# Mask product one phase after its exponentials, row turns in later steps, a fourth PSUM bank from the fusion on, and batch 1's dilated turns by DMA

## The chip, the cores and the metric

The kernel runs on one core of one Trainium2 chip. The metric is the device time of one execution in microseconds (us). The kernel before took 256.71 us, the median of 7 runs (256.2 to 257.37).

## The reference

Windowed attention over 8 batches, 8 heads, 576 positions and 64 dimensions a head, followed by a multiplicative feed-forward network over the 4608 tokens. Heads 0 to 3 see the last 32 positions ("plain"), heads 4 to 7 every fourth of the last 128 ("dilated").

```python
scores = scale * np.matmul(q, k.transpose(0, 1, 3, 2))
mask_plain = (rel >= 0) & (rel < window)
mask_dil = (rel >= 0) & (rel < window * dilation) & (rel % dilation == 0)
scores = np.where(masks[None, :, :, :], scores, -1000000000.0)
attn = np.exp(scores - np.max(scores, axis=-1, keepdims=True))
attn = attn / (np.sum(attn, axis=-1, keepdims=True) + 1e-09)
x = np.matmul(attn, v)      # to (4608, 512), heads side by side
a = x @ w1                  # 512 -> 1024
b = x @ w2
out = (a * b @ w3) @ w_out  # 1024 -> 1024 -> 512
```

## The kernel before, in words

The instructions are placed by hand: each engine executes what it is given in the order in which the program issues it. TensorE's stream is the feed-forward network of one batch; the attention of a later batch is cut into small phases that are put between its matmuls.

*The network.* `ffn1(b, hf, f)` makes one 128 x 288 block of a * b: four matmuls with w1 into a PSUM bank, a cast to `asb` on ScalarE (L612), four with w2 into another bank, and on VectorE the gate product of the bank and `asb` into `gt` (L619). Its matmuls (L579) read `XT[1]` (dilated heads, chunks 2 and 3) first and `XT[0]` (plain heads) after. `ffn2` multiplies 128 tokens by the fused weights (L646), ScalarE copies the bank to `osb` (L653, six buffers) and SP's queue stores it. The fused weights w3 w_out are made once, by `fuse_t` (turns of w3 on TensorE, copied by ScalarE) and `fuse_m` (L676, copied to `wf_sb` by VectorE at L684). Batch 0's ffn1 runs until about 37 us with banks of its own. Then come the fusion (to 55.7 us), batch 0's first four ffn2 tiles (to about 64 us), and from there ffn1 of batches 1 to 7 with the ffn2 tiles that come due, some 27 us a batch.

*Banks.* `bank()` gives out the banks of a pool of three in turn. From the moment `late["x"]` is set, every fourth call gives `ps_x`, a bank set aside. Before the change this is set after batch 1. Until then `ps_x` serves `fuse_t(0)` and the turns in `to_channels`, and for the turns it goes on doing so.

*The attention.* A `Step` is one batch, one kind of heads (u = 1 dilated, 0 plain) and one half of the positions; a batch has the four steps d0, d1, p0, p1. `transposes` turns rows of q and k (loaded by POOL's queue) so that the head dimension lies on partitions, by VectorE (L277, L269): four pieces each for q and dilated k, two for plain k. `scores` issues 24 small matmuls into `ps_a`, their exponentials into `et` on ScalarE (L343), and the product with the 0/1 mask in place on VectorE (L344). `values` multiplies `et` by v (L355), and VectorE takes reciprocals (L363) and scales into `xo` (L366, five buffers). `to_channels` turns `xo` into `XT`: by six turns on TensorE (L413) into `ps_x` and a copy by ScalarE (L419), or, where `by_dma` is set, by one transposing DMA on SP's queue (L404). Before the change that is for batches above 2 and the dilated steps of batch 2.

*Phases.* `later(f)` makes a phase and `behind(f)` adds to the last one. `second_batch` lists the phases of batch 1 with the point at which each is issued; `segment` makes those of batches 2 to 7. In `segment` each phase has a width (`after`), and `point(n)`, called before each product of ffn1 (0.57) and each half of an ffn2 tile or of a `fuse_m` (1), counts points and issues all phases that are due. A batch is 27.25 points. `marks` fixes by which point each batch's last step must be done; `ahead` moves that point earlier. Phase by phase, a step in `segment` is: its scores; an empty phase with two row turns behind it; the turns of the step two back; the values of the step before; an empty phase with two more row turns. `prefetch` issues the loads of a batch that is two ahead.

Of the kernel before, what the change touches and what calls it, by code (L numbers as in the profile page):

```python
# [12 lines left out]
BF16 = mybir.dt.bfloat16  # L13
# [3 lines left out]
ACT = mybir.ActivationFunctionType  # L17
# [6 lines left out]
HALF = 288  # L24
# [29 lines left out]
def kernel(  # L54
# [11 lines left out]
    nc = tc.nc  # L66
# [6 lines left out]
    KFF = d_ff // P  # L73
    NT = n_tok // TB
    scale = 1.0 / float(np.sqrt(D))
# [42 lines left out]
    ps_x = psum.tile([P, 2 * TB], BF16, name="ps_x")  # L118
    pool = four_banks()
    ps_s = [pool.tile([P, 2, TB], F32, name=f"ps_s{i}") for i in range(2)]  # L120
    late = {}

    def bank():
        if "x" in late:
            late["x"] += 1
            if late["x"] % 4 == 0:
                return ps_x.bitcast(F32)
        return banks.tile([P, TB], F32, tag="f", name="f")
# [163 lines left out]
    class Step:  # L292
        def __init__(self, n, b, u, hf):
            self.b, self.u, self.hf = b, u, hf
            self.et = ets[n % NET]

            self.by_dma = b > 2 or (b == 2 and u == 1)
            self.xo = {}

        def score_matmuls(self, heads, bank_of, start):  # L300
# [36 lines left out]
        def scores(self):  # L337

            ps_a = late["a"]
            self.score_matmuls(range(4), lambda h: ps_a[:, h], True)  # L340
            ev = self.probs(0, 4)
            mk = (mask_di if self.u else mask_pl[:, self.hf]).rearrange("p m x -> p (m x)")
            nc.scalar.activation(out=ev, in_=ps_a[:, :, 0:HALF], func=ACT.Exp, scale=scale)  # L343
            nc.vector.tensor_tensor(  # L344
                out=ev, in0=ev, in1=mk.unsqueeze(1).to_broadcast([P, 4, HALF]), op=AL.mult
            )
# [51 lines left out]
                        self.value_matmul(2 * hp + hl, m, ov[:, j // 3, j % 3, :])  # L398
            self.normalize(ov, self.xo.rearrange("p h j d -> p (h j) d"), 4, 3)()

        def to_channels(self, ps=ps_x, copy=nc.scalar.copy, hps=(0, 1)):
            dst = XT[self.u][:, 2 * self.b + self.hf]
            if self.by_dma:
                nc.sync.dma_start(  # L404
                    out=dst.rearrange("p h (m t) -> p (h m) t", m=3),
                    in_=self.xo[0:96].rearrange("p h (m e) d -> p (h m) (e d)", m=3),
                    transpose=True,
                )
                return
            xv = ps[:, 0 : 2 * HALF].rearrange("p (h x) -> p h x", h=2)  # L410
            for hp in hps:
                for m in range(3):
                    nc.tensor.transpose(  # L413
                        out=xv[:, hp, 96 * m : 96 * m + 96],
                        in_=self.xo[0:96, hp, 2 * m : 2 * m + 2, :],
                        identity=ident[0:96, 0:96],
                    )
            h = slice(hps[0], hps[-1] + 1)
            copy(out=dst[:, h], in_=xv[:, h])  # L419
# [3 lines left out]
    steps = [  # L423
        Step(4 * b + 2 * (1 - u) + hf, b, u, hf)
        for b in range(B)
        for u in (1, 0)
        for hf in range(2)
    ]
# [10 lines left out]
    def later(f, *args, after=1.0):  # L439

        phases.append([lambda: f(*args)])
        room.append(after)
# [5 lines left out]
    def first_batch():  # L448


        d0, d1, p0, p1 = steps[0:4]
        transpose_qk(0, 1, 0)
        transpose_qk(0, 1, 1)
        d0.scores_of_pair(0)
        d0.scores_of_pair(1)
        transpose_qk(0, 0, 0)
        d1.scores_of_pair(0)
        d1.scores_of_pair(1)
        transpose_qk(0, 0, 1)
        warm_up(4)  # L460
        p0.scores_of_pair(0)
        p0.scores_of_pair(1)
        warm_up(2)
        d0.values_of_pair(0)
        d0.values_of_pair(1)
        p1.scores_of_pair(0)
        warm_up(1)
        d1.values_of_pair(0)
        d1.values_of_pair(1)
        p1.scores_of_pair(1)  # L470
        d0.to_channels()
        p0.values_of_pair(0)
        p1.values_of_pair(0)
        pool = four_banks()
        ps_b = [pool.tile([P, TB], F32, name=f"ps_b{i}") for i in range(4)]
        late.update(b=ps_b, n=0)
        d1.to_channels(ps_b[0].bitcast(BF16))
        warm_up(1, ps_b[3])
        p0.values_of_pair(1)
        p0.to_channels(ps_x, hps=(0,))  # L480
        p1.values_of_pair(1)
        begin(0, 0, (2, 3))
        begin(0, 1, (2, 3))
        begin(0, 0, (0,))
        begin(0, 1, (0,))
        p0.to_channels(ps_x, hps=(1,))
        x1 = bank().bitcast(BF16)
        p1.to_channels(x1, nc.vector.tensor_copy, hps=(0,))
        begin(1, 0, (2, 3))
        begin(1, 1, (2, 3))  # L490
        begin(0, 0, (1,))
        begin(0, 1, (1,))
        p1.to_channels(x1, nc.vector.tensor_copy, hps=(1,))
        begin(1, 0, (0,))
        begin(1, 1, (0,))
        ffn1(0, 0, 0)
        begin(1, 0, (1,))
        begin(1, 1, (1,))
        const_masks()
        prefetch(2)  # L500
# [3 lines left out]
    def second_batch():  # L504

        d0, d1, p0, p1 = steps[4:8]
        for at, f, *args in (
            (19, transpose_qk, 1, 1, 0),
            (20, transpose_qk, 1, 1, 1),
            (22, d0.scores),  # L510
            (24, d1.scores),
            (26, d0.values),
            (26, transpose_qk, 1, 0, 0),
            (27, transpose_qk, 1, 0, 1),
            (28, d0.to_channels),
            (28, d1.values),
            (31, p0.scores),
            (32, d1.to_channels),
            (33, p1.scores),
            (35, p0.values),  # L520
            (37, p0.to_channels),
            (37, p1.values),
            (37, prefetch, 3),
            (37, transpose_qk, 2, 1, 0),
            (38, transpose_qk, 2, 1, 1),
            (39, p1.to_channels),
            (39, transpose_qk, 2, 0, 0),
        ):
            later(f, *args)
            when.append(at)  # L530

    def segment(lo, hi):


        pieces = []

        def some():
            for f in pieces[:2]:
                behind(f)
            del pieces[:2]  # L540

        for i in range(lo, hi + 1):
            at, b = i % 4, i // 4
            more = 4 * (b + 1) < hi
            if at == 0 and i < hi:
                pieces += transposes(b, 0, 1)
                for u, which in ((1, 0), (1, 1), (0, 0)) if more else ():
                    pieces += transposes(b + 1, u, which)
            if i < hi:
                later(steps[i].scores, after=0.8)  # L550
                later(lambda: None, after=0.8)
                some()
            if i > lo + 1 and not steps[i - 2].by_dma:
                later(steps[i - 2].to_channels, after=0.4)
                done_at[i - 2] = len(phases)
            if i > lo:
                later(steps[i - 1].values, after=0.8)
                if steps[i - 1].by_dma:
                    behind(steps[i - 1].to_channels)
                done_at[i - 1] = len(phases)  # L560
                if i < hi:
                    later(lambda: None, after=0.8)
                    some()
            if at == 2:
                behind(prefetch, b + 2)

# [89 lines left out]
    w3T = {}  # L656

    def fuse_t(ft):
        xv = bank().bitcast(BF16) if ft else ps_x
        xv = xv.rearrange("p (g x) -> p g x", g=KFF)  # L660
        for g in range(KFF):
            nc.tensor.transpose(  # L662
                out=xv[:, g, :],
                in_=w3n[ft // 2][:, ft % 2, g * P : (g + 1) * P],
                identity=ident,
            )
        w3T[ft] = wk_pool.tile([P, KFF, P], BF16, tag="w3T", bufs=3, name="w3T")
        nc.scalar.copy(out=w3T[ft], in_=xv)
# [44 lines left out]
    n0 = len(when)  # L713
    marks = [(40, n0)]
    for b in range(2, B):
        ahead = (0, 3, 6)[min(b - 2, 2)]
        marks.append((40 + 27.25 * (b - 1) - ahead, done_at[4 * b + 3]))
    place = np.concatenate([[0.0], np.cumsum(room)])
    xs, ys = [m[0] for m in marks], [place[m[1]] for m in marks]
# [1 line left out]
    def point(n):  # L721
        state[0] += n
        want = int(np.searchsorted(place, np.interp(state[0], xs, ys) - 1e-6))
        while state[1] < want and (state[1] >= n0 or state[0] >= when[state[1]]):
            for f in phases[state[1]]:
                f()
            state[1] += 1

    for f in range(1, KFF + 2):
        if f < KFF:  # L730
            ffn1(0, 0, f)
        if f == KFF:
            fuse_t(0)
        if f >= 2:
            ffn1(0, 1, f - 2)
# [14 lines left out]
    for b in range(1, B):  # L750
        for hf in range(2):
            for f in range(KFF):
                ffn1(b, hf, f, point)
                if due and f in (1, 3, 5):
                    ffn2(due.pop(0), point)
            while P * (done + 1) <= b * S + (hf + 1) * HALF:
                due.append(done)
                done += 1
        if b == 1:
            late["x"] = 0  # L760
    for t in due:
        ffn2(t, point)
    assert state[1] == len(phases)
# [30 lines left out]
```

## Time and profile before

| | us |
|---|---|
| median of 7 runs | 256.71 (256.2 to 257.37) |
| the profiled execution | 256.57 |
| its span | 254.8 |
| TensorE, scores of one step (24 matmuls) | 0.44 |
| exponentials of one step, L343 | 1.13 |
| mask product, L344 | 0.76 |
| gate product, L619 | 0.50 |
| cast of a bank, L612 | 0.40 |
| reciprocals and scaling, L363 and L366 | 0.22 and 0.95 |
| row turn, L277 (q and dilated k) | 0.42 |
| copy of six turns, L419 | 0.64 |

Busy time of the engines by stage, and what the DMA engines moved (the share is the sum of packet times over 16 engines, so that it can go above one):

| stage, us | TensorE | VectorE | ScalarE | POOL | DMA share | GB/s |
|---|---|---|---|---|---|---|
| 40.0 to 55.7 | 15.41 | 11.96 | 9.73 | 8.75 | 1.42 | 198 |
| 55.7 to 68.3 | 12.34 | 9.38 | 7.52 | 6.19 | 1.50 | 217 |
| 68.3 to 95 | 26.42 | 20.04 | 13.38 | 6.13 | 1.73 | 187 |
| 95 to 122 | 27.00 | 18.10 | 12.99 | 5.48 | 0.98 | 146 |
| 122 to 149 | 27.00 | 19.30 | 12.82 | 5.48 | 0.94 | 135 |
| 149 to 176 | 27.00 | 18.57 | 12.96 | 4.07 | 0.69 | 100 |

A matmul's record runs from its start to its end, and the next one starts before that end; so an engine that waits a little between two matmuls can still be counted as busy. The distance between starts tells more than the busy share. In the waits, a line reads: engine and line that waited, what it waited for, us in total, number of times, longest.

### The profile page before, as it was taken

Reading aid. Unit: us, or ns where it says so; the run is one execution under the profiler, and the core shown is the slowest. Engines: PE = TensorE matmul, PEld = TensorE weight load, DVE = VectorE, ACT = ScalarE, POOL = GpSimd, SP = SyncE. Lnnn points to the kernel's source line nnn. Section 1 sums busy time; section 2 is a strip of 40 time slices with the busy share of each in tenths; the row PEclk is TensorE's granted clock in tenths of the full one; section 3 lists DMA queues with packets and bytes.
Section 4 is the critical chain, followed back from the end, with each engine's and each line's share of the span. In section 5 each row is a group of like instructions: output and inputs, shape, how many; then the busy total and the mean of one; then the engine's idle time right before and its main releaser. Section 6 shows DMA issues by size and latency. Waiting matters only on the chain.

```text
span 254.8 us, 6683 instructions
## 1 busy us (share of the span) xinstructions
PE 249.2 (98%) x2700; PEld 165.4 (65%) x2700; DVE 160.9 (63%) x379; ACT 119.3 (47%) x220; POOL 59.9 (23%) x87
## 2 busy tenths in 40 slices
PE   7999999999999999999999999999999999999995
PEld 2467774645676766667676766676767666777663
DVE  6676436867878766657685866576767543645550
ACT  2464456564644554554545454454444445333332
POOL 8884333747206200511061106000000000000000
PEclk9999999999999999999999999999999999999999
DMA  6999999999999993999479968922314122312113
GB/s 103 166 186 199 207 213 198 190 203 199 256 192 141 174 221 106 134 185 155 111 101 164 177 106 124 169 67 44 88 26 104 48 64 67 106 32 76 41 44 123
DMA packets 66562, 33.81 MB, mean 133 GB/s; under 512 B 51556, under 2 KB 56932, under 8 KB 66532
## 3 DMA queue, kind: packets, MB, share of 16 engines
q0 software_dynamic: 47232, 20.70, 69.0%
q1 hardware_dynamic: 19300, 12.69, 20.0%
q8 instruction: 21, 0.34, 0.6%
q14 instruction: 9, 0.07, 0.1%
HBM read 41.39 MB, written 9.44 MB: 199 GB/s over the span
## 4 chain that ended last, share of the span: by engine, by line
PE 78%; DMA 12%; DVE 3%; ACT 2%; POOL 2%; issue 1%; POOLq 0%
PE f L579 32%; PE f L646 19%; PE ps_x L579 9%; DMA qn<-in_q_dram 6%; PE ps_x L646 5%; PE ps_a L355 4%; PE f L676 4%; PE ps_a L313 4%; DMA w_sb<-in_moe_w_dram 3%; DMA kn<-in_k_dram 2%; ACT et L343 2%; POOL w_sb L177 1%; PE f L662 1%; PE ps_x L413 1%; DVE gt L619 1%
## 5 line engine op out<-in xcount | busy, mean ns | idle before, releaser
L579 PEld LDWEIGHTS <-w_sb 128*128 128x128 bf16 x1024 | 97.2, 98 | 30.9 <-issue 2.0
L579 PE MATMUL f<-XT,w_sb 128*128 128x288 bf16 x704 | 100.5, 286 | 0.5 <-DVE gt L619 0.2
L619 DVE TENSOR_TENSOR gt<-f,asb 128x288 bf16<-128x288 f32 x91 | 45.1, 503 | 17.9 <-PE f L579 17.8
L646 PE MATMUL f<-wf_sb,gt 128*128 128x512 bf16 (+1 forms) x240 | 55.9, 372 | 0.0
L612 ACT CAST asb<-f 128x288 bf16<-128x288 f32 x85 | 33.9, 399 | 33.4 <-PE f L579 31.1
L646 PEld LDWEIGHTS <-gt 128*128 128x128 bf16 x296 | 27.7, 98 | 25.5
L343 ACT ACTIVATE et<-ps_a 128x1152 bf16<-128x1152 f32 x28 | 31.7, 1131 | 10.4 <-PE ps_a L313 10.4
L653 ACT COPY osb<-f 128x512 f32<-128x512 f32 (+1 forms) x30 | 17.1, 571 | 39.8 <-PE f L646 37.7
L166 POOL DMA_DIRECT2D vd<-in_v_dram x32 | 21.3, 673 | 53.0 <-PE ps_a L355 46.2
L579 PE MATMUL ps_x<-XT,w_sb 128*128 128x288 bf16 x192 | 31.4, 286 | 0.0
L366 DVE TENSOR_TENSOR xo<-ps_a,rcp 96x768 bf16<-96x768 f32 x28 | 26.7, 954 | 1.0
L344 DVE TENSOR_TENSOR et<-et,mask_pl 128x1152 bf16<-128x1152 bf16 x14 | 10.6, 758 | 19.2 <-ACT et L343 19.2
L277 DVE STREAM_TRANSPOSE qt<-qn 128x160 uint32<-128x160 uint32 (+1 forms) x64 | 21.2, 422 | 2.3 <-DMA qn<-in_q_dram 2.2
L344 DVE TENSOR_TENSOR et<-et,mask_di 128x1152 bf16<-128x1152 bf16 x14 | 10.6, 758 | 17.8 <-ACT et L343 17.8
L355 PEld LDWEIGHTS <-et 128*128 128x128 bf16 x384 | 16.0, 98 | 3.4 <-ACT et L333 0.2
L313 PEld LDWEIGHTS <-kt 32*128 32x128 bf16 x768 | 10.6, 93 | 11.4 <-issue 8.6
L579 PE MATMUL ps_b<-XT,w_sb 128*128 128x288 bf16 x128 | 16.5, 286 | 0.0
L612 ACT CAST asb<-ps_x 128x288 bf16<-128x288 f32 x27 | 10.8, 398 | 11.2 <-PE ps_x L579 11.2
L676 PE MATMUL f<-wo_sb,w3T 128*128 128x512 bf16 x64 | 16.0, 380 | 0.0
L646 PE MATMUL ps_x<-wf_sb,gt 128*128 128x512 bf16 x56 | 13.2, 379 | 0.0
L619 DVE TENSOR_TENSOR gt<-ps_x,asb 128x288 bf16<-128x288 f32 x21 | 10.1, 483 | 4.3 <-PE ps_x L579 4.3
L313 PE MATMUL ps_a<-qt,kt 32*128 32x96 bf16 x672 | 12.4, 202 | 0.3 <-DVE kt L277 0.3
(71 smaller groups left out, 179.2 us busy)
## 6 DMA issues: line engine op xcount, KB each, us to landing
out_dram<-osb SPq DMA_DIRECT2D x28, 144.0 KB
qn<-in_q_dram POOLq DMA_DIRECT2D x6, 576.0 KB, 9.9
kn<-in_k_dram POOLq DMA_DIRECT2D x6, 576.0 KB, 10.3
w_sb<-in_moe_w_dram POOLq DMA_DIRECT2D x8, 256.0 KB, 7.9
w3n<-in_moe_w_dram POOLq DMA_DIRECT2D x4, 512.0 KB, 14.0
vp<-in_v_dram POOLq DMA_DIRECT2D x5, 384.0 KB, 7.4
out_dram<-osb SPq DMA_DIRECT2D x10, 128.0 KB
qn<-in_q_dram POOLq DMA_DIRECT2D x4, 288.0 KB, 6.6
```

What stands on the lines that cost most here:

```text
L166: nc.gpsimd.dma_start(out=vds[b % 2][p0 : p0 + n, 4 * m : 4 * m + 4, 16 : 16 + 2 * D], in_=bass.AP(tensor=x.tensor, offset=x.offset + (4 * ...
L277: nc.vector.transpose(out=bass.AP(tensor=o.tensor, offset=o.offset + at, ap=[o.ap[0], [1, n], [9, 16], [step, 2]],), in_=t[:, k : k + 4 * ...
L313: nc.tensor.matmul(out=bank_of(h)[:, c0 : c0 + 96], lhsT=kt[prt, 96 * m : 96 * m + P, c], rhs=rhs, start=(start and c == 0), stop=(c == 1 ...
L343: nc.scalar.activation(out=ev, in_=ps_a[:, :, 0:HALF], func=ACT.Exp, scale=scale)
L344: nc.vector.tensor_tensor(out=ev, in0=ev, in1=mk.unsqueeze(1).to_broadcast([P, 4, HALF]), op=AL.mult)
L355: nc.tensor.matmul(out=out, lhsT=self.et[:, c0 : c0 + P], rhs=rhs, start=True, stop=True)
L366: nc.vector.tensor_tensor(out=xo[0:96].rearrange("p (n k) d -> p n k d", n=n), in0=ov[0:96, :, :, x0 : x0 + D], in1=rcp[0:96].unsqueeze(3) ...
L579: nc.tensor.matmul(out=ps[:, 0:HALF], lhsT=w_sb[:, c, f * P : (f + 1) * P], rhs=x, start=(c == 2), stop=(c == 1),)
L612: nc.scalar.copy(out=a_sb, in_=ps[:, 0:HALF])
L619: nc.vector.tensor_tensor(out=g, in0=pb, in1=a_sb, op=AL.mult)
L646: nc.tensor.matmul(out=y, lhsT=gt[:, f, g0 : g0 + P], rhs=wf_sb[:, f, c0 : c0 + n], start=(f == 0), stop=(f == KFF - 1),)
L676: nc.tensor.matmul(out=wf_ps[ft], lhsT=w3T[ft][:, g, :], rhs=wo_sb[:, g, :], start=(g == 0), stop=(g == KFF - 1),)
```

## The change

Five edits.

1. The mask product leaves `scores` and becomes a phase of its own, `mask`, where the empty phase after the scores was (in batch 1 it gets points of its own, one after those of the scores).
2. The row turns of a batch's four steps, before two behind each of the two empty phases, are issued in the numbers (2, 0), (0, 2), (3, 3), (2, 2): the first number behind the scores, the second at the end of the step.
3. `late["x"]` is set before the loop of batch 0's ffn1, so that the fusion, batch 0's first ffn2 tiles and batch 1's ffn1 have four banks in turn. `fuse_t(0)` and the turns of `to_channels` take their bank from the rotation.
4. The dilated steps of batch 1 are turned by DMA.
5. `ahead` of batch 3 is 4 points where it was 3.

```diff
-            self.by_dma = b > 2 or (b == 2 and u == 1)
+            self.by_dma = b > 2 or (b > 0 and u == 1)
...
             ev = self.probs(0, 4)
+            nc.scalar.activation(out=ev, in_=ps_a[:, :, 0:HALF], func=ACT.Exp, scale=scale)
+
+        def mask(self):
+            ev = self.probs(0, 4)
             mk = (mask_di if self.u else mask_pl[:, self.hf]).rearrange("p m x -> p (m x)")
-            nc.scalar.activation(out=ev, in_=ps_a[:, :, 0:HALF], func=ACT.Exp, scale=scale)
             nc.vector.tensor_tensor(
...
-        def to_channels(self, ps=ps_x, copy=nc.scalar.copy, hps=(0, 1)):
+        def to_channels(self, ps=None, copy=nc.scalar.copy, hps=(0, 1)):
...
+            if ps is None:
+                ps = bank().bitcast(BF16)
...
             (22, d0.scores),
+            (23, d0.mask),
             (24, d1.scores),
+            (25, d1.mask),
...
             (32, d1.to_channels),
+            (32, p0.mask),
             (33, p1.scores),
+            (34, p1.mask),
...
-        def some():
-            for f in pieces[:2]:
+        def some(n):
+            for f in pieces[:n]:
                 behind(f)
-            del pieces[:2]
+            del pieces[:n]
...
+            n = ((2, 0), (0, 2), (3, 3), (2, 2))[at]
             if i < hi:
                 later(steps[i].scores, after=0.8)
-                later(lambda: None, after=0.8)
-                some()
+                some(n[0])
+                later(steps[i].mask, after=0.8)
...
                 if i < hi:
                     later(lambda: None, after=0.8)
-                    some()
+            if i < hi:
+                some(n[1])
...
-        xv = bank().bitcast(BF16) if ft else ps_x
-        xv = xv.rearrange("p (g x) -> p g x", g=KFF)
+        xv = bank().bitcast(BF16).rearrange("p (g x) -> p g x", g=KFF)
...
-        ahead = (0, 3, 6)[min(b - 2, 2)]
+        ahead = (0, 4, 6)[min(b - 2, 2)]
...
+    late["x"] = 0
     for f in range(1, KFF + 2):
...
-        if b == 1:
-            late["x"] = 0
```

Left out: `first_batch` now names `ps_x` in its one call of `to_channels` that had it by default, so nothing changes there.

More of the change, by code (lines that the diff above doesn't have):

```diff
@@ L470, in first_batch @@
         p1.scores_of_pair(1)
-        d0.to_channels()
+        d0.to_channels(ps_x)
         p0.values_of_pair(0)
```

## The prediction

> **What bounds the kernel now.** I read the page's shares first, then who waited for whom, then TensorE's own timeline, and the chain last, to see where the timeline's gaps stop.
>
> ```profile
> PE 249.2 (98%) x2700; PEld 165.4 (65%) x2700; DVE 160.9 (63%) x379; ACT 119.3 (47%) x220; POOL 59.9 (23%) x87
> ...
> PEclk9999999999999999999999999999999999999999
> ```
>
> TensorE is called busy for 98% of the span at the full clock, so only its own work or gaps hidden inside its busy time can give anything back.
>
> ```profile
> DVE et L344 <- ACT et L343: 37.0, 27, 2.8
> ```
>
> VectorE stood 37.0 us, in 27 waits, with a mask product at the head of its queue whose exponentials were not done: 1.37 us each. Everything behind it waits too, such as the gate products (L619) that free a PSUM bank. What that costs must be read on TensorE.
>
> ```profile
> 41.51 1.04 PE L676 MATMUL f<-wo_sb,w3T 128*128 128x512 bf16 x4
> 42.54 0.62 PE L662 MATMUL f<-ident,w3n 128*128 128x128 bf16 x8
> ...
> 49.06 0.42 PE L413 MATMUL ps_x<-ident,xo 96*128 96x96 bf16 x6
> 49.31 0.53 PE L355 MATMUL ps_a<-vd,et 128*128 128x65 bf16 x12
> ...
> 64.29 2.34 PE L579 MATMUL f<-XT,w_sb 128*128 128x288 bf16 x16
> 66.56 0.44 PE L313 MATMUL ps_a<-qt,kt 32*128 32x96 bf16 x24
> 66.94 1.15 PE L579 MATMUL f<-XT,w_sb 128*128 128x288 bf16 x8
> 68.30 1.79 PE L579 MATMUL f<-XT,w_sb 128*128 128x288 bf16 x12 [0.21 <-DVE gt L619]
> 69.92 0.53 PE L355 MATMUL ps_a<-vd,et 128*128 128x65 bf16 x12
> 70.29 2.28 PE L579 MATMUL f<-XT,w_sb 128*128 128x288 bf16 x16
> 72.51 0.44 PE L313 MATMUL ps_a<-qt,kt 32*128 32x96 bf16 x24
> 72.88 3.11 PE L579 MATMUL f<-XT,w_sb 128*128 128x288 bf16 x20
> ...
> 91.22 1.89 PE L646 MATMUL f<-wf_sb,gt 128*128 128x512 bf16 x8
> 93.18 0.41 PE L413 MATMUL ps_x<-ident,xo 96*128 96x96 bf16 x6
> ```
>
> Each line is a run of matmuls: start, length, count. Undisturbed, a 288-column matmul starts every 0.1225 us (four in 0.49) and the last one shows 0.286, so a run of n should last 0.1225 n + 0.16; a 512-column one starts every 0.216.
>
> ```profile
> 126.32 1.47 PE f L579 x12
> 127.79 0.49 PE ps_x L579 x4
> ```
>
> These are such undisturbed lines of the chain (12 x 0.1225 = 1.47, the next run follows at once). From 95 us to the end I find no start late by over 0.04 us. There bank() already hands out four banks, ps_x among them. Before 95 us the runs are too long.
>
> **The change, part by part.**
>
> *Fourth bank from the fusion on, and the mask a phase later.* The excess, run by run: 42.54 should have been 41.51 + 4 x 0.216 = 42.37, so 0.16; the run at 64.29, 2.34 against 2.12, 0.21; 68.30 against 66.94 + 0.98, 0.37; inside the run at 68.30, 1.79 against 1.63, 0.16; at 70.29, 0.16; at 72.88, 3.11 against 2.61, 0.49 in two stalls; two more runs at 83.90 and 87.69, 0.21 and 0.12 by the same sum; and 93.18 should have been 91.22 + 1.73, so 0.23. The sum is 2.11 us. The stalled matmuls waited for ScalarE's casts or for VectorE, that is, for a bank. With a fourth bank each asks for its bank one product (0.49 us) later, and no single stall is longer than 0.37. The mask product moves behind at least part of the work that it held up. I count 2.11 gained; bounds 1.0 (if the waits for VectorE, about half of it, come back elsewhere) and 2.11. After 95 us the later mask gains nothing, because TensorE shows no gap there to fill. A fifth stall, 0.35 at 41.13, waits for the row turns of batch 1, which wait for a load until 39.02; it stays.
>
> *Batch 1's dilated turns by DMA.* Two groups of six turns leave TensorE: 49.06 to 49.31, 0.25 each, 0.50 together, both behind the load-bound point at 41.13, so on the path. Two copies of 0.64 leave ScalarE, which gains nothing by itself. Added are two issues on SP's queue, which has nothing to do between 44 and 58.20 us, the first store. The stores queue behind the turns: their first rows land from 61.87 now, and up to 3 us later does not matter, since six osb buffers let the seventh tile, at about 93 us, be the first to wait. Batch 1's first product at 64.29, earlier by 0.16 + 0.50, so 63.6, needs both turns, its first two chunks being the dilated ones. The xo of the second is written as follows:
>
> ```profile
> 51.36 0.95 DVE L366 TENSOR_TENSOR xo<-ps_a,rcp 96x768 bf16<-96x768 f32 x1
> ```
>
> That ends at 52.31 (the first at 48.30). No turn runs so early now; the nearest are batch 2's two, issued at 71.74 and 77.76 into rings just as full: their last packets ended 10.4 and 7.4 us later, the first packet 4.0 us after issue, and the packets took 6.4 and 3.1 us. An undisturbed one (217.79) took 2.1. For batch 1: the first starts moving at 52.3 and ends between 55.4 and 58.7; the second, behind it, ends between 59.5 and 65.1. While q/k loads run (2304-byte packets until 57.6) the slow figure applies, after it the fast one: I take 61.5, 2 us before the need. Cost nothing; bounds 0 and 1.5.
>
> The Trainium skill (VectorE: DVE Perf Modes, Rules for kernel authors) speaks against this part: turn a full block on TensorE where PSUM may take it, by DMA otherwise. By it the two turns should stay, and the sum lose the 0.50. The trace here shows TensorE as the full engine, so I do not follow the rule.
>
> Its page DMA: Bandwidth & Descriptors (Latency and other measured facts) gives 261 GB/s for such a transfer; its 147 KB would take an estimated 0.56 us, and by that no turn could be late. The trace's 3.1 and 6.4 us beside loads differ, and I use those.
>
> *Load traffic.* The two turns delay the loads beside them. During the turn that ended at 85.17 the vd loads moved 320 packets in 2.7 us where 0.6 is usual, so I price a turn at 0.9 (its packets alone, 218.97 to 219.84) to 2 us of ring time, 2 to 4 for both. Batch 2's k rows land at 57.6 and are turned from 62.5; batch 3's k rows land at 69.64, and their first turn moves up from 75.21 to right behind the q turns, about 71.5. The first has 4.9 us of cover, the second 1.9. Value: 0; bounds 0 and 1.6.
>
> *Row turns to later steps.* Same turns, 0.31 to 0.46 each. The third step of a batch gets six where it had four. VectorE is busy 18 to 20 of 27 us in these stages and loses its 1.37 us waits, which is the cover; without it two turns, 0.6 us, would stand before a gate product and cost about 0.1 beyond the 0.49 of a bank. POOL's q load of the batch after next is released some 3.4 us later (83.84 now, landed 92.73, next read about a batch later): nothing.
>
> *Plain turns of batches 1 and 2 in the rotation* instead of a bank apart: between 0 and the 0.23 of the 93.18 row, for the two in batch 2; I take 0.1 in all. *ahead 3 to 4* ends batch 3's attention one point (about 1 us) earlier in a stage without gaps: nothing.
>
> Sum: -2.11 - 0.50 + 0.1 = -2.5 us. The profiled execution took 256.57 (span 254.8 and 1.8 around it) and lies 0.14 below the median. So 254.07 in its terms, 254.2 against the median of 256.71.
>
> **The rivals.**
>
> *Loads decide, and part is given back.* Batch 3's k rows come 3.6 us later, at 73.2, VectorE waits 1.6 us for them with gate products queued behind, and TensorE runs out of banks for up to 1.6. Or the second turn lands at 65.1, TensorE waiting 1.5. Either gives 255.8. For it: the DMA share is above one from 40 to 95 us. Against it: the covers above.
>
> *The mask was never the cost.* The waits for VectorE return at the next bank, and the gain is the casts' share (1.0) and the turns (0.50): 255.2. Against it: after 95 us the same masks wait just as long with four banks, without one late matmul.
>
> *Slower: the second turn lands far too late.* Its place is batch 1's first product. If it too needed 10.4 us after the first had landed (48.3 + 10.4 = 58.7), it would be there at 69.1; TensorE would stand 5.5 us, the gain of 2.5 would be lost, and the time would be 259.7. It decides from a landing at 66.6 on (63.6 plus 2.5 plus 0.5), 14.3 us after xo. For it: kn loads took 11.2 us in these rings. Against it: no turn took over 10.4.
>
> **How the numbers follow.** Forecast 0.66; loads 0.12; mask 0.10; slower 0.12. The likeliest case itself spans 253.7 to 254.8. The range 253.6 to 255.9 takes in the next two rivals and leaves out the slower one. A difference under 0.2%, 0.5 us, can't be told from none here; a little of the loads' case, where both prices meet, falls inside it: faster 0.81, same 0.07, slower 0.12.
>
> **What would show it.** Right: no run of L579 between 62 and 95 us longer than its count allows; the waits of et on ACT near 0 and VectorE waiting on products instead; the six-turn groups near 49 and 54 us gone; batch 1's first product at about 63.6 with no idle before it; everything after 95 us the same, 2.5 us earlier. Wrong: TensorE idle before that product on XT's DMA, VectorE idle before kt on the kn load near 72 us, or new late runs after 95 us where the third step has six row turns.

## The result and the profile after

The changed kernel takes 260.00 us (median of 23 runs, 257.34 to 262.31) against 257.11 (60 runs) for the one before: 1.0097 times as long, 95% interval 1.0077 to 1.0117. Here and below a time is the median of all runs, while a ratio and its interval leave out the few runs more than 1.5% above the fastest of their kernel, so the two need not divide exactly. The change is slower by 1%, where 1% less was forecast. The profiled execution took 260.63 with a span of 258.8, against 254.8 before; the account below is of that 4.0 us. The spans of all its executions lie between 255.6 and 260.5 us, and the longer ones have the lower clock in the mean (0.999 or 1.0 up to 257.3 us, 0.987 to 0.993 from 258.2 on), so the last loss below, the half clock, differs from one execution to the next.

From the page of the changed kernel, busy shares and granted clock:

```profile
PE 249.6 (96%) x2688; PEld 165.8 (64%) x2688; DVE 163.2 (63%) x379; ACT 118.1 (46%) x218; POOL 59.9 (23%) x87
...
PEclk9999999999999869999999999999999999999999
```

TensorE has 12 matmuls fewer, the two groups of turns, yet its share fell from 98% to 96%, and in the 14th and 15th of 40 slices (84 to 97 us) its clock is below full. The waits say what for (engine, line, what it waited for, total, number, longest):

```profile
DVE et L347 <- ACT et L342: 3.8, 6, 1.0
PE f L591 <- DMA XT<-xo: 3.7, 1, 3.7
```

The first is VectorE's mask product: 3.8 us in 6 waits where it was 37.0 in 27. The second, TensorE's, did not exist before. Where it lies is seen on TensorE's timeline (start, length, instructions, and in brackets the idle time before and what ended it):

```profile
62.95 0.67 PE L591 MATMUL f<-XT,w_sb 128*128 128x288 bf16 x4
...
71.14 1.64 PE L591 MATMUL f<-XT,w_sb 128*128 128x288 bf16 x12
73.22 0.65 PE L591 MATMUL ps_x<-XT,w_sb 128*128 128x288 bf16 x4 [0.44 <-DVE gt L631]
...
85.85 0.65 PE L591 MATMUL f<-XT,w_sb 128*128 128x288 bf16 x4
90.17 2.08 PE L591 MATMUL f<-XT,w_sb 128*128 128x288 bf16 x8 [3.66 <-DMA XT<-xo]
92.04 1.16 PE L591 MATMUL ps_x<-XT,w_sb 128*128 128x288 bf16 x4
93.14 0.67 PE L313 MATMUL ps_a<-qt,kt 32*128 32x96 bf16 x24
93.74 1.14 PE L591 MATMUL f<-XT,w_sb 128*128 128x288 bf16 x4
94.67 2.26 PE L658 MATMUL f<-wf_sb,gt 128*128 128x512 bf16 x8
96.77 0.42 PE L418 MATMUL f<-ident,xo 96*128 96x96 bf16 x6
```

Batch 1's first product is at 62.95 and has no wait. Then there are three losses. The run at 73.22 should have begun at 71.14 + 12 x 0.1225 = 72.61: 0.61 late. Batch 2's first product was due at 85.85 + 0.49 = 86.34 and began at 90.17: 3.83 late. And from there on everything is stretched: four matmuls last 1.16 where 0.65 is usual, 24 scores 0.67 where 0.44. The granted clock is half of full from 88.59 to 95.41.

What released the two late runs is in the chain of waits (start, length, piece):

```profile
58.03 14.37 DMA kn<-in_k_dram
...
72.42 0.04 DVE kt L277
...
72.74 0.44 DVE gt L631
...
73.22 0.65 PE ps_x L591 x4
...
75.71 14.32 DMA XT<-xo
90.03 0.14 issue
90.17 2.08 PE f L591 x8
```

Batch 3's k rows are in flight for 14.37 us and are released to VectorE at 72.40 (their last packet ends at 72.06); the row turn waits for them at the head of VectorE's queue, the gate product is behind it, and TensorE runs out of banks. This is the load rival's first half. The second late run waits for a DMA turn, but not for one of the two that the change added: those were issued at 47.51 and 51.33 and had landed by 59.30, 3.6 us before use. It is *batch 2's* second dilated turn, a DMA turn in both kernels. Issued at 75.71, its packets run from 80.38 to 89.44. Before, it was issued at 77.76, its packets ran from 82.09 to 85.17, and it was needed at 88.67: 3.5 us of cover.

By rings the text means the queues of the core's 16 DMA engines taken together. What they did then shows in the table by stage (window, its length, busy time of TensorE, its weight loads, VectorE, ScalarE and POOL with counts, clock, DMA share, GB/s). The changed kernel:

```profile
70.00:75.00 5.00, 4.56 (x67) 3.42 (x66) 4.07 (x13) 2.54 (x5) 0.75 (x2) 1.00 1.69 193
75.00:80.00 5.00, 5.00 (x64) 3.15 (x63) 4.38 (x11) 2.47 (x5) 3.50 (x5) 1.00 3.47 72
80.00:85.00 5.00, 5.00 (x62) 3.40 (x61) 4.00 (x9) 2.81 (x6) 0.70 (x1) 1.00 1.93 141
...
90.00:95.00 5.00, 4.83 (x41) 2.80 (x42) 0.47 (x2) 1.93 (x3) 0.00 (x0) 0.50 1.98 199
```

The kernel before:

```profile
75.00:80.00 5.00, 4.89 (x64) 3.06 (x63) 3.82 (x11) 2.16 (x4) 3.23 (x5) 1.00 1.32 195
80.00:85.00 5.00, 5.00 (x66) 3.31 (x64) 3.51 (x9) 2.31 (x5) 1.54 (x2) 1.00 2.41 101
```

From 75 to 80 us the packets were in flight for more than twice as long in sum (share 3.47 against 1.32), and moved little more than a third (72 against 195 GB/s): most of the time in flight was waiting. Everything in these rings came later:

| load, issue to the end of its last packet | before | after |
|---|---|---|
| k rows of batch 3 | 58.40 to 69.64 | 58.03 to 72.06 |
| plain v of batch 3 | 61.73 to 75.30 | 62.26 to 82.20 |
| q rows of batch 4 | 65.08 to 76.75 | 65.61 to 83.87 |
| k rows of batch 4 | 68.25 to 81.54 | 69.47 to 88.93 |

The account of the span: gained are all the late starts of before after 40 us, 2.11 + 0.35 = 2.46, and 0.50 of turns. Lost are 0.61, 3.83, and the half clock: from 90.17 to 96.77 is 6.60 us for work that takes 4.16 at the full clock (86.67 to 90.83 in the first experiment's timeline below), so 2.44. Net 6.88 - 2.96 = 3.92 of the 4.0. Two more differences nearly cancel: TensorE began batch 0's first product 0.30 earlier than before (17.82 against 18.11), and from the start of the last matmul of ffn1 to the end 0.4 more passed (8.9 against 8.5).

### The profile page after: what moved, and what is told of

Same layout as the page of the kernel before. It is cut to its first block, busy times and chain, and to the rows that moved or that the text cites. A ratio compares the mean times of both kernels' runs of the same rounds, so it can differ in the third digit from the quotient of the medians.

```text
span 258.8 us, 6670 instructions
## 1 busy us (share of the span) xinstructions
PE 249.6 (96%) x2688; PEld 165.8 (64%) x2688; DVE 163.2 (63%) x379; ACT 118.1 (46%) x218; POOL 59.9 (23%) x87
## 4 chain that ended last, share of the span: by engine, by line
PE 83%; DMA 13%; DVE 1%; issue 1%; ACT 0%; POOL 0%; POOLq 0%; DVEq 0%
PE f L591 28%; PE f L658 16%; PE ps_x L591 10%; DMA kn<-in_k_dram 7%; PE ps_b L591 6%; DMA XT<-xo 6%; PE ps_x L658 5%; PE f L687 5%; PE ps_a L313 3%; PE ps_a L358 3%; PE ps_s L313 1%; PE f L673 1%; PE ps_s L329 1%; PE ps_x L687 1%; PE ps_x L205 1%
## 5 line engine op out<-in xcount | busy, mean ns | idle before, releaser
L591 PE MATMUL f<-XT,w_sb 128*128 128x288 bf16 x672 | 98.3, 289 | 3.7 <-DMA XT<-xo 3.7
L631 DVE TENSOR_TENSOR gt<-f,asb 128x288 bf16<-128x288 f32 x86 | 43.7, 510 | 39.6 <-PE f L591 33.5
L658 PE MATMUL f<-wf_sb,gt 128*128 128x512 bf16 (+1 forms) x216 | 51.7, 377 | 0.0
L591 PE MATMUL ps_x<-XT,w_sb 128*128 128x288 bf16 x224 | 37.1, 289 | 0.4 <-DVE gt L631 0.4
L665 ACT COPY osb<-f 128x512 f32<-128x512 f32 (+1 forms) x27 | 15.6, 577 | 39.1 <-PE f L658 39.1
L631 DVE TENSOR_TENSOR gt<-ps_x,asb 128x288 bf16<-128x288 f32 x26 | 12.4, 478 | 12.3 <-PE ps_x L591 7.6
L624 ACT CAST asb<-ps_x 128x288 bf16<-128x288 f32 x30 | 12.0, 400 | 14.0 <-PE ps_x L591 14.0
L658 PE MATMUL ps_x<-wf_sb,gt 128*128 128x512 bf16 (+1 forms) x80 | 18.2, 369 | 0.0
L687 PE MATMUL f<-wo_sb,w3T 128*128 128x512 bf16 x56 | 13.9, 379 | 0.0
L366 DVE RECIPROCAL rcp<-ps_a 96x12 f32<-96x12 f32 x28 | 6.3, 224 | 12.0 <-PE ps_a L358 11.9
```

The costliest lines, as they stand in the source:

```text
L591: nc.tensor.matmul(out=ps[:, 0:HALF], lhsT=w_sb[:, c, f * P : (f + 1) * P], rhs=x, start=(c == 2), stop=(c == 1),)
L624: nc.scalar.copy(out=a_sb, in_=ps[:, 0:HALF])
L631: nc.vector.tensor_tensor(out=g, in0=pb, in1=a_sb, op=AL.mult)
L658: nc.tensor.matmul(out=y, lhsT=gt[:, f, g0 : g0 + P], rhs=wf_sb[:, f, c0 : c0 + n], start=(f == 0), stop=(f == KFF - 1),)
L665: nc.scalar.copy(out=o_sb[:, c0 : c0 + n], in_=y)
L687: nc.tensor.matmul(out=wf_ps[ft], lhsT=w3T[ft][:, g, :], rhs=wo_sb[:, g, :], start=(g == 0), stop=(g == KFF - 1),)
```

## The experiments

The theory that they test: the two new transfers back up the rings, so that batch 2's second turn and batch 3's k rows land late, and the rest of the change gains what was forecast or more. The rivals stand in each expectation.

**1. All but the new turns by DMA.** The changed kernel, with batch 1's dilated turns on TensorE again.

```diff
-            self.by_dma = b > 2 or (b > 0 and u == 1)
+            self.by_dma = b > 2 or (b == 2 and u == 1)
```

> The changed kernel with batch 1's dilated turns back on TensorE (by_dma as before); the other four edits stay. Ring theory (the two added turns push loads and batch 2's own DMA turns back): batch 2's second turn lands by 86 us, TensorE does not wait for XT before batch 2's first product, the clock stays at 1.0, and the time is 2 us below the kernel before (ratio 0.990 to 0.995). Rival (the row turns in later steps release the loads later and bunch them with batch 2's turns): the wait on XT stays, 1 us or more, and the ratio is 1.00 or above. Second rival (TensorE simply arrives too early for turns that land where they always did): a wait of about 1 us stays and the ratio is 0.995 to 1.00.

254.21 us (6 runs), ratio 0.9876 (0.9839 to 0.9913), span 252.5, full clock throughout. TensorE's timeline around batch 2's first product:

```profile
85.69 1.14 PE L591 MATMUL f<-XT,w_sb 128*128 128x288 bf16 x8
86.67 0.65 PE L591 MATMUL ps_x<-XT,w_sb 128*128 128x288 bf16 x4
87.16 1.14 PE L591 MATMUL f<-XT,w_sb 128*128 128x288 bf16 x8
88.23 0.44 PE L313 MATMUL ps_a<-qt,kt 32*128 32x96 bf16 x24
...
89.10 1.89 PE L658 MATMUL ps_x<-wf_sb,gt 128*128 128x512 bf16 x8
90.83 0.42 PE L418 MATMUL f<-ident,xo 96*128 96x96 bf16 x6
```

The same work as in the changed kernel from 85.36 on, 0.3 us later than there and with no gap: batch 2's first product is at 86.67. Its second turn was issued at 75.92, within 0.3 us of the changed kernel's, and landed at 83.56 instead of 89.44. The rings from 75 to 80 us:

```profile
75.00:80.00 5.00, 5.00 (x66) 3.29 (x64) 4.26 (x11) 2.71 (x5) 3.83 (x5) 1.00 1.37 197
```

197 GB/s against 72. The issue time is nearly the same, and only two transfers some 25 us earlier are missing; so this loss comes from them, not from the other edits. This version beats both kernels, and by more than was expected (0.990 at best).

**2. The new turns alone**, in the kernel before.

```diff
-            self.by_dma = b > 2 or (b == 2 and u == 1)
+            self.by_dma = b > 2 or (b > 0 and u == 1)
```

> The kernel before with one edit alone, batch 1's dilated turns by DMA. Ring theory: batch 2's second turn lands 2 to 4 us later than in the kernel before (85.2 us there), near 88, close to its need near 88.5; the ratio is 1.000 to 1.012, some executions with a wait on XT. Rival (row turns to later steps): no wait on XT, batch 2's turns land where they did, 0.5 us of TensorE is saved and the ratio is 0.998.

262.18 us (6 runs), ratio 1.0194 (1.0140 to 1.0249). TensorE's timeline:

```profile
90.65 1.63 PE L579 MATMUL f<-XT,w_sb 128*128 128x288 bf16 x12 [2.29 <-DMA XT<-xo]
...
120.32 0.90 PE L579 MATMUL f<-XT,w_sb 128*128 128x288 bf16 x6 [1.09 <-DMA XT<-xo]
...
147.31 0.40 PE L579 MATMUL f<-XT,w_sb 128*128 128x288 bf16 x2 [0.86 <-DMA XT<-xo]
```

Three waits for turns, in the first products of batches 2, 3 and 4: the delay comes back from batch to batch. So this one edit costs more than the whole change does, and more than was expected (1.012 at most). The clock of this profiled execution is full; four of the other five have means of 0.985 to 0.993.

**3. Batch 2's dilated turns on TensorE**, batch 1's by DMA: the late transfer is taken away, the added ones stay.

```diff
-            self.by_dma = b > 2 or (b > 0 and u == 1)
+            self.by_dma = b > 2 or (b == 1 and u == 1)
```

> The changed kernel with the turns of batch 2's dilated steps on TensorE, those of batch 1 by DMA. Ring theory: no turn stands in the full rings when batch 2's first product needs it, the wait before that product is gone, the clock stays at 1.0 and the ratio is 0.990 to 0.995; the wait for batch 3's k rows near 72 us (0.6 us) stays, as batch 1's turns still delay the loads. If the loss is in the loads themselves, a wait of over 1 us for a load shows elsewhere and the ratio is 1.00 or above.

255.77 us (12 runs), ratio 0.9945 (0.9911 to 0.9979). No wait for `XT`. Batch 3's k rows are still late, on VectorE:

```profile
73.98 0.46 DVE L277 STREAM_TRANSPOSE kt<-kn 128x160 uint32<-128x160 uint32 x1 [1.73 <-DMA kn<-in_k_dram]
```

TensorE is 2.05 us late behind it at 74.78, and then its clock halves (column before the last two), for 0.17 x 10 / 0.5 = 3.4 us:

```profile
75.00:85.00 10.00, 10.00 (x103) 6.35 (x101) 7.26 (x18) 3.89 (x7) 4.07 (x5) 0.83 1.55 189
```

This execution is one of two among the 12 with a mean clock of 0.993; the other ten have 0.998 or more. The run also tells which transfers slow one another down: batch 1's two turns are there, batch 2's are not, and the rings move 189 GB/s. The collapse goes with a turn that lies among loads that are behind; the 101 GB/s of the kernel before from 80 to 85 us, during its own turn, look like the same on a smaller scale.

**4. TensorE kept busy in the gap.** Sixteen matmuls on a constant tile ahead of batch 2's first product, which only add to the work.

```diff
+            if b == 2 and hf == 0:
+                warm_up(16, bank())
             for f in range(KFF):
                 ffn1(b, hf, f, point)
```

> The changed kernel with 16 extra matmuls of 512 columns (3.5 us, on constants) in front of batch 2's first product; their products are not used. If the half clock from 90 to 95 us comes from TensorE standing idle for 3.8 us, the clock stays at 1.0 in every stage, the wait shrinks to under 1 us and the time is about 2 us below that of the changed kernel (ratio 1.002 to 1.004 where that has 1.010). If the clock falls for another reason, the half clock stays and the ratio is 1.010 or above.

259.36 us (10 runs), ratio 1.0076 (1.0048 to 1.0104). The filler occupies TensorE from 87.39 to 90.84, the turn lands at 89.03 under it, and the clock stays full in every execution (mean 0.998 or more). So the half clock follows from standing still, not from the work behind it. The time expected, 1.002 to 1.004, was not reached, and the interval overlaps that of the changed kernel: the filler's own 3.45 us take the place of the gap, and what the half clock costs the median is not settled by this run. In the changed kernel itself the 9 executions with a mean clock of 0.998 or more have a median of 258.7 us, the 14 with a lower one 260.6; their gaps may differ in length too. Even at the full clock it is slower than the kernel before.

**5. The fourth bank alone**, in the kernel before (edit 3).

```diff
-        def to_channels(self, ps=ps_x, copy=nc.scalar.copy, hps=(0, 1)):
+        def to_channels(self, ps=None, copy=nc.scalar.copy, hps=(0, 1)):
...
+            if ps is None:
+                ps = bank().bitcast(BF16)
...
-        xv = bank().bitcast(BF16) if ft else ps_x
-        xv = xv.rearrange("p (g x) -> p g x", g=KFF)
+        xv = bank().bitcast(BF16).rearrange("p (g x) -> p g x", g=KFF)
...
+    late["x"] = 0
     for f in range(1, KFF + 2):
...
-        if b == 1:
-            late["x"] = 0
```

> The kernel before with the fourth bank from the fusion on, alone (mask, row turns, DMA turns as before). If the bank covers each late start by itself, no run of L579 between 62 and 95 us is too long and the ratio is 0.990 to 0.993, as with all four edits but the DMA turns (0.988). If the mask product's wait was the cost, half of the 2.1 us of late starts stay and the ratio is 0.994 to 0.997.

255.71 us (12 runs), ratio 0.9952 (0.9927 to 0.9978). VectorE still waits 35.9 us for exponentials, yet the late starts before 95 us shrink from 2.46 to 0.34 us, so the bank covers nearly all of them by itself; the ratio is nevertheless in the range of the other case (0.994 to 0.997). One new wait comes after them:

```profile
115.81 0.90 PE L581 MATMUL f<-XT,w_sb 128*128 128x288 bf16 x6 [0.95 <-DMA XT<-xo]
```

It is batch 3's first plain chunk, whose turn was issued at 107.45 and landed at 115.27. TensorE arrives earlier, the transfer does not.

**6. The later mask alone**, in the kernel before (edit 1).

```diff
             ev = self.probs(0, 4)
+            nc.scalar.activation(out=ev, in_=ps_a[:, :, 0:HALF], func=ACT.Exp, scale=scale)
+
+        def mask(self):
+            ev = self.probs(0, 4)
             mk = (mask_di if self.u else mask_pl[:, self.hf]).rearrange("p m x -> p (m x)")
-            nc.scalar.activation(out=ev, in_=ps_a[:, :, 0:HALF], func=ACT.Exp, scale=scale)
...
-                later(lambda: None, after=0.8)
+                later(steps[i].mask, after=0.8)
```

> The kernel before with the mask product one phase later, alone (three banks until the end of batch 1). If the bank is what counts, VectorE's waits for the exponentials fall from 37 us to under 5, yet most late starts stay and the ratio is 0.995 to 1.000. If the mask's wait was the cost, the starts that waited for VectorE (about 1 us) are gone and the ratio is 0.992 to 0.996.

256.75 us (12 runs), ratio 0.999 (0.996 to 1.002). VectorE's waits for exponentials fall to 7.7 us, and seven late starts from 0.16 to 0.67 us stay. Almost 30 us of waits taken off VectorE are worth nothing measurable.

**7 and 8. Is it the turning or the bytes?** Experiment 1, in which batch 1's dilated blocks are in addition sent by SP's queue to tiles that nobody reads: in 7 by a transposing DMA, in 8 by a plain copy of the same bytes in 256-byte pieces.

```diff
+            if self.b == 1 and self.u == 1:
+                nc.sync.dma_start(
+                    out=scr[self.hf].rearrange("p h (m t) -> p (h m) t", m=3),
+                    in_=self.xo[0:96].rearrange("p h (m e) d -> p (h m) (e d)", m=3),
+                    transpose=True,
+                )
             if ps is None:
```

Experiment 8 has `out=scr[self.hf][0:96, :, 0:P]` and no `transpose`.

> The changed kernel with batch 1's dilated turns on TensorE, and in addition the same two DMA turns from the same xo into scratch tiles that nothing reads. Ring theory: the two transfers alone delay batch 2's turns, TensorE waits 2 to 4 us for XT before batch 2's first product, and the ratio is 1.000 to 1.012 where it is 0.988 without them. If the loss needs batch 1's product to depend on the turns, or TensorE's earlier arrival, the ratio stays at 0.988 to 0.992.

> As the kernel with scratch turns, but with two plain copies of the same bytes in pieces of 256 bytes in place of the turns. If the bytes and packets fill the rings, the loss is that of the scratch turns (ratio 1.000 to 1.012). If it is the turning that slows the transfers beside it, the copies cost little: no wait on XT of over 0.5 us, ratio 0.987 to 0.993.

With turns 260.98 us (6 runs), ratio 1.0121 (1.0077 to 1.0164); with copies 259.94 (11 runs), 1.0075 (1.0041 to 1.0110). Both wait for batch 2's second turn, which lands at 89.36 and 89.66. From the timeline of the turns:

```profile
90.19 0.91 PE L598 MATMUL ps_x<-XT,w_sb 128*128 128x288 bf16 x4 [2.75 <-DMA XT<-xo]
```

and of the copies:

```profile
90.60 1.12 PE L597 MATMUL ps_x<-XT,w_sb 128*128 128x288 bf16 x4 [3.32 <-DMA XT<-xo]
```

Transfers that nobody waits for turn the gain of 1.2% into a loss of 0.8 to 1.2%, and plain copies do it too: it is the traffic of the added transfers, not their transposing and not the dependence on them.

**9. The fourth bank and `ahead`**, in the kernel before (edits 3 and 5), to see whether an earlier end of batch 3's attention removes the wait of experiment 5.

```diff
...
-        ahead = (0, 3, 6)[min(b - 2, 2)]
+        ahead = (0, 4, 6)[min(b - 2, 2)]
```

> The kernel before with the fourth bank and ahead 4 for batch 3 (edits 3 and 5), mask, row turns and DMA turns as before. With the bank alone the one late start left was 1.1 us at batch 3's first product, waiting for the turn of a plain step; if one point of lead covers it, the ratio is 0.987 to 0.991, as with all edits but the DMA turns (0.988), and mask and row turns are worth nothing by themselves. If the row turns' later order (which moves the q load) covers it, the wait stays and the ratio is 0.993 to 0.996.

255.81 us (12 runs), ratio 0.9968 (0.9933 to 1.0002). Batch 3's wait is gone and 0.70 us has come up at batch 4's (141.78). The time is that of experiment 5 and not the 0.991 or less that was expected, so the two edits are not all of experiment 1's gain.

**10. Experiment 1 with the row turns where they were** (edits 1, 3 and 5).

```diff
-            n = ((2, 0), (0, 2), (3, 3), (2, 2))[at]
...
-                some(n[0])
                 later(steps[i].mask, after=0.8)
+                some()
...
                     later(lambda: None, after=0.8)
+                    some()
-            if i < hi:
-                some(n[1])
```

> Bank, mask a phase later and ahead 4, with batch 1's turns on TensorE and the row turns in their old places (edits 1, 3, 5). If the row turns' order is worth something, through the q load that it releases later, TensorE waits for XT or the ratio is 0.003 or more above 0.988. Otherwise 0.987 to 0.990.

256.32 us (12 runs), ratio 0.9974 (0.9949 to 0.9999). Batch 3's wait is back:

```profile
117.50 0.90 PE L589 MATMUL f<-XT,w_sb 128*128 128x288 bf16 x6 [1.00 <-DMA XT<-xo]
```

Here the q load of batch 6 is issued at 107.79, ahead of batch 3's plain turn (108.54), which lands at 116.78. In experiment 1 the later row turns release that load at 108.74, behind the turn (106.76), which lands at 111.26. The moved row turns thus give about 1%. This place has 1.16 us of the 2.6 between the two profiled spans (255.1 against 252.5); two late starts, 0.39 at 69.03 and 0.24 at 87.64, come with it, and the rest is open. That the order of the two transfers makes the place late is read from the two traces; no run changes that order alone.

**11. The changed kernel with batch 4's loads held back** until the second of batch 2's turns has landed: a small POOL copy ahead of them reads what that turn writes.

```diff
             issued.add(b)
+            if b == 4:
+                nc.gpsimd.tensor_copy(out=gate, in_=XT[1][:, 5, 0, 0:2])
             load_qk(b)
```

> The changed kernel with one small POOL copy in front of batch 4's loads that reads the block of XT written by batch 2's second turn, so that POOL issues these loads only when that turn has landed. Ring theory (the turn is late because it shares the rings with batch 3's and 4's loads): batch 2's second turn lands by 84 us instead of 89.4, no wait on XT before batch 2's first product, and the ratio is 0.986 to 0.990; loads of batch 4 come by 100 us, before their row turns. If the lateness comes from SP's own queue or from the turns themselves, it stays at 87 us or later and the ratio at 1.00 or above.

255.65 us (12 runs), ratio 0.9943 (0.9919 to 0.9968). The turns are issued at 70.03 and 76.02, within 0.4 us of the changed kernel's, and land at 76.01 and 78.38: the second takes 2.4 us where it took 13.7, and there is no wait for `XT`. What slows it in the changed kernel is these loads in the same rings. The ratio expected, 0.986 to 0.990, was not reached; the profile shows 0.56 us late at 73.54 for batch 3's k rows, and where the rest of the difference to experiment 1 lies is open.

**12. Experiment 1 with the mask behind its exponentials again** (edits 2, 3 and 5).

```diff
-                later(steps[i].mask, after=0.8)
+                later(lambda: None, after=0.8)
```

with the mask product back at the end of `scores`.

> Bank, row turns in later steps and ahead 4, with the mask product right behind its exponentials and batch 1's turns on TensorE (edits 2, 3, 5). If the later mask is worth nothing with four banks, the ratio is 0.987 to 0.990 and VectorE's waits for the exponentials are back at 35 us or so with no late start on TensorE. If it matters, late starts of 0.5 us or more in sum appear where six row turns stand in one step, ratio 0.990 to 0.994.

257.01 us (12 runs), ratio 1.0008 (0.9984 to 1.0031). VectorE's waits for exponentials are back at 35.9 us, and TensorE's timeline has this:

```profile
87.01 0.42 PE L415 MATMUL ps_x<-ident,xo 96*128 96x96 bf16 x6 [1.02 <-DVE gt L624]
```

VectorE's timeline shows what stands ahead of that gate product:

```profile
84.74 0.76 DVE L344 TENSOR_TENSOR et<-et,mask_di 128x1152 bf16<-128x1152 bf16 x1 [1.73 <-ACT et L342]
85.42 1.25 DVE L269 STREAM_TRANSPOSE kt<-kn 128x288 uint32<-128x288 uint32 x2
86.51 0.44 DVE L624 TENSOR_TENSOR gt<-ps_x,asb 128x288 bf16<-128x288 f32 x1
```

The mask waits 1.73 us for its exponentials, and the two row turns that edit 2 puts behind the scores follow at once. Here the waits behind exponentials do cost: the start at 87.01 is 1.18 us late, and others between 0.22 and 0.58. The place is not the step with six row turns that was expected but one with two, those of plain k, 0.62 us each; and the cost is higher than expected (0.994 at most). So the later mask, worth nothing alone, is what lets the row turns lie where they lie.

**Together.** Edits 1, 2, 3 and 5 are worth 0.9876; the bank alone 0.9952, the mask alone nothing, and each of the four trials that leave out part of the set (5, 9, 10, 12) is above 0.995. Edit 4 takes 1.0097 / 0.9876, 2.2%, or 5.7 us. Why a turn among loads that are behind moves at a third of the rate was not tried further.

## Why the prediction was wrong

*The step that failed* is the cost of the added transfers: "Load traffic ... Value: 0; bounds 0 and 1.6". It asked what the two turns do to batch 1's first product and to the k rows of batches 2 and 3, and left out the two transfers in the same rings with a due time of their own, batch 2's dilated turns. Their figures were in hand: the second ended at 85.17 and was needed at 88.67, 3.5 us of cover. It was even used as the example of a slow turn in full rings. Of the 2 to 4 us of ring time that the text itself priced for both turns, the upper end uses up that cover and 0.5 us more, so batch 2's first product belonged among the places asked about. The runs show 3.83 of lateness and 2.44 of half clock behind it, and 0.61 for batch 3's k rows (1.01 in experiment 4, whose instructions are the same up to there): 6.9 us in place of 0. Experiments 1, 7, 8 and 11 show that it is those transfers among these loads.

*The figure of ring time* (0.9 to 2 us a turn) was also too small. It is what a turn occupies, not what it does to rings that are already behind: the loads of the table came 2.4, 6.9, 7.1 and 7.4 us later, and batch 2's second turn took 13.7 us from issue to its last packet, against 7.6 in experiment 1. Nor did the cover shrink because TensorE came earlier: in experiment 1 the turn came earlier with it, and 3.1 us of cover are left (83.56 to 86.67).

*The half clock* was in no case of the prediction; with TensorE never idle, the profile of before could not show it. The Trainium skill (TensorE: Matmul & The Clock Gate, Why this matters for your kernels) says to have no idle gaps above some 3 us in TensorE's stream, or the rate drops to half. The 3.83 us here agree. Experiment 3 differs: 2.05 us late, and 3.4 us of half clock, while the 2.46 us in the profiled execution of experiment 2 were followed by none. The measurements decide: a shorter gap can be enough, and the same length need not be. The traces show what separates them. The granted clock changes only on a grid of 3.41 us, counted from the first clock record of each trace (75.52 and 78.93 in experiment 3; 88.59 and 95.41, two steps apart, in the changed kernel). TensorE's idle time within the step ahead of each half clock was 1.89 us in experiment 3, 2.08 and 1.58 in the changed kernel, 2.75 and 2.85 in experiments 7 and 8. In experiment 2 a grid point at 89.68 splits the gap into 1.32 and 0.97, and the clock stays full, as it does after every step of the 14 traces with 1.32 or less. So the limit lies between 1.32 and 1.58 us idle in one step, as far as these traces go; no run was made to test it.

*Fourth bank and later mask, 2.11, bounds 1.0 to 2.11*: right. The 0.35 at 41.13, which was to stay, is gone in this execution, but experiment 4, with the same instructions there, has 0.24 at that place: it differs from one execution to the next. "With a fourth bank each asks for its bank one product (0.49 us) later" is what experiment 5 shows, in which 2.12 of the 2.46 us go, the 0.35 among them. That the mask gains nothing by itself is experiment 6. What the later mask gives is the cover for the row turns, VectorE's lost waits, which the text named; only the price without it was too small: 0.1 us beside the 1.3% between experiments 1 and 12. It took 0.6 us for two turns, and the two of plain k in experiment 12 take 1.25.

*Batch 1's turns, 0.50, cost 0*: right in its own place. They landed at 59.30 where 61.5 was taken, and the product came at 62.95 without a wait (63.6 predicted).

*Row turns 0; POOL's q load "released some 3.4 us later ... nothing"*: wrong in sign. With the later release the q load of batch 6 falls behind batch 3's plain turn, and the 1.16 us of experiment 10 are not there.

*`ahead`, nothing*: the 1.11 us wait of experiment 5 is gone in experiment 9, but the times of the two do not differ.

*The rivals.* "Loads decide" came true for the k rows, with 0.61 of the 1.6 us. Of "the mask was never the cost", experiment 6 shows the first half, but the waits for VectorE do not return at the next bank (experiment 5), and 1.0 of gain was too little. The slower rival had the right mechanism, a turn that lands far too late, but put it at batch 1's first product, with 5.5 us of standing and no half clock. That its 259.7 lies near the 260.00 is luck. It ought to have been asked of every turn in the stage.

## What to carry to other kernels

A transfer added to shared rings is priced by everything that is already due in them: list each transfer of that stage with its landing and its need, and in rings that are behind expect a delay of several times what the new ones occupy alone (here up to 7.4 us, for two turns whose packets take 0.9 each when nothing is in the way). An engine that stands behind another for 37 us may be worth nothing by itself; the bank was worth 0.5% alone and the mask nothing, but the set of four 1.2%, of which most was lost without the mask or without the row order. Once an idle gap of over 1.3 us opens in TensorE's stream, price half clock behind it as well: here one or two steps of 3.41 us, 1.7 us lost in a full one.

## What was not expected of the hardware

A turn of 256-byte pieces on SP's queue beside loads on POOL's queue that are behind: from 75 to 80 us the rings moved 72 GB/s instead of 195, and 128-byte packets took 304 to 368 ns in the mean of each us from 77 to 80, where 32 is usual. Two plain copies of such pieces, some 25 us earlier, put the loads behind as far as two turns do: batch 4's k rows end at 89.10 and 89.04 in experiments 8 and 7, against 81.63 in experiment 1. The same turn took 2.4 us from issue to landing with the loads held back and 13.7 among them. And TensorE's clock was halved for 3.4 us after a start only 2.05 us late, and not after one 2.46 us late whose gap was split between two steps of the clock's grid.
